# Reordering the opening transposes, filler matmuls and copies out of PSUM of an attention and feed-forward kernel

## The chip, the cores and the metric

The kernel runs on one core of one Trainium2 chip. The metric is the device time of one execution in microseconds (us). A kernel's executions are given as median and range. The profile that goes with a kernel is of one execution, and its span is about 1.8 us shorter than that execution's time, because the span begins with the first recorded instruction. All executions told of here were in the same state ("fast"); the profile gives the clock that TensorE was granted, and where it was below full speed (1.0) this is said.

In the lines of the profile PE is TensorE (matmuls), PEld its weight loads, DVE is VectorE, ACT is ScalarE, POOL is GpSimd and SP is SyncE; a `q` after an engine's name means the engine's sequencer, which issues and waits. L144 is line 144 of the kernel. PSUM is the memory that TensorE writes its results to.

## The reference

```python
def _attn_ref(x, state):                 # x (8, 8, 512, 64), state (8, 8, 32, 64)
    scores = scale * (x @ state^T);  a  = softmax(scores);   xread = a @ state
    scores2 = scale * (state @ x^T); a2 = softmax(scores2);  sread = a2 @ x
    return concat([xread, sread], axis=2)

def reference(x, state, w_in, w_out):
    y = attn.transpose(0, 2, 1, 3).reshape(8 * 544, 512)
    h = y @ w_in                         # 512 -> 2048
    g = h * sigmoid(h)
    return g @ w_out                     # 2048 -> 512
```

(Shortened to the mathematics; the maxima that the softmaxes subtract are left out.)

## The kernel before

Eight batches go through one TensorE queue. Each batch's scores need x transposed (`xT`), and the first product of the feed-forward part needs the normalised scores transposed (`aT`). For batches 0 and 1 these transposes are made by TensorE, with a copy out of PSUM behind each. For batches 2 to 7 they are made by DMA, issued from the SyncE queue. While inputs arrive, TensorE runs filler matmuls on zeros so that its clock is released (in the trace of before, at 5.63 us).

```python
def warm(n, bk, w=128):                                   # filler
    for i in range(n):
        nc.tensor.matmul(bank[bk][:, 0:w], zeros[:, 0:128], zeros[:, 0:w], ...)

def x_T(b, kt, bk):                                       # L144: x transposes on TensorE
    for c in range(4):
        nc.tensor.transpose(v[:, kt % 2, c, :], x_n[b % 2][:, kt, c, ds(2, 128)], ident[:])

def x_Te(b, kt, n, bk, eng):                              # L84 / L88: their copy
    cp(eng, xT[b % 2][:, ds(kt, n)], v[:, ds(kt % 2, n)])

def a_T(b, bks):                                          # L230: batches 0 and 1
    ...
            cp(e, aT[b % 2][:, ds(i * n, n)], v[:, ds(0, n)])

def a_Td(b):                                              # L236: batches 2 to 7
    nc.sync.dma_start_transpose(aT[b % 2]..., an[b % 2]...)

# [cut] the schedule, start of batch 0
warm(30, "o0")
# [cut]
warm(3, "w1")
x_T(0, 1, XB[1]); x_Te(0, 1, 1, XB[1], "act"); cast2(0, 3)
# [cut] loads
sc(0, 0, SB[0]);  ex(0, 0, 1, SB[0])
warm(4, "w1")
sc(0, 1, SB[1]);  ex(0, 1, 1, SB[1])
x_T(0, 2, XB[2]); x_Te(0, 2, 1, XB[2], "act")
red(0); red(1)
x_T(0, 3, XB[3]); x_Te(0, 3, 1, XB[3], "dve")
```

`sc` are scores, `ex` exponentials on ScalarE, `red` sums on VectorE of one pair of heads, and `cast2` casts one pair of heads of x as it lands.

The softmax here doesn't subtract the row's maximum and nothing guards it: scores larger than these inputs give would overflow.

Of the kernel before, what the change touches and what calls it, by code (L numbers as in the profile page):

```python
# [19 lines left out]
def kernel(  # L20
# [58 lines left out]
    def bf(name):  # L79
        return bank[name][:].bitcast(BF16)  # L80

    def cp(eng, dst, src):
        if eng == "dve":
            nc.vector.tensor_copy(dst, src)  # L84
        elif eng == "pool":
            nc.gpsimd.tensor_copy(dst, src)  # L86
        else:
            nc.scalar.activation(dst, src, func=COPY, bias=0.0)  # L88
# [43 lines left out]
    def st_f32(bk, e0, e1):  # L132
        v = bf(bk)[:, 0:128]
        for half, e in ((0, e0), (1, e1)):
            cp(
                e,
                sbd_f[ds(64 * half, 64)],
                v[ds(64 * half, 64)].rearrange("p (ns kt) -> p kt ns", kt=KT),
            )

    def x_T(b, kt, bk):
        v = bf(bk).rearrange("p (k c t) -> p k c t", k=2, c=4)
        for c in range(4):
            nc.tensor.transpose(  # L144
                v[:, kt % 2, c, :], x_n[b % 2][:, kt, c, ds(2, 128)], ident[:]
            )

    def x_Te(b, kt, n, bk, eng):
        v = bf(bk).rearrange("p (k c t) -> p k c t", k=2, c=4)
        cp(eng, xT[b % 2][:, ds(kt, n)], v[:, ds(kt % 2, n)])  # L150
# [22 lines left out]
    def sc(b, kt, bk):  # L173
        v = bank[bk][:].rearrange("p (k h c s) -> p k h c s", k=2, h=2, c=4)
        for c in range(4):
            nc.tensor.matmul(  # L176
                v[:, kt % 2, :, c, :],
                xT[b % 2][:, kt, c, :],
                sbd[:, b, kt, :, :],
                start=True,  # L180
                stop=True,
                skip_group_check=True,
            )

    def ex(b, kt, n, bk):
        v = bank[bk][:].rearrange("p (k q s) -> p k q s", k=2, q=8)
        nc.scalar.activation(  # L187
            en[b % 2][:, :, :, ds(kt, n), :].rearrange("p h c k s -> p k (h c) s"),
            v[:, ds(kt % 2, n)],
            func=EXP,  # L190
            bias=0.0,
            scale=SCALE,
        )
# [6 lines left out]
    def norm_m(b, eng, kt=0, n=4, h0=0, hn=2):  # L200
        e = nc.vector if eng == "dve" else nc.gpsimd
        e.tensor_tensor(  # L202
            an[b % 2][:, ds(h0, hn), :, ds(kt, n), :].rearrange("p h c k s -> p (h c) k s"),
            en[b % 2][:, ds(h0, hn), :, ds(kt, n), :].rearrange("p h c k s -> p (h c) k s"),
            rs[b % 2][:, ds(h0, hn), :, ds(kt, n)]
            .rearrange("p h c k -> p (h c) k")
            .unsqueeze(3)
            .to_broadcast([128, 4 * hn, n, NS]),
            op=MULT,
        )  # L210

    def norm_g(b, eng, kt, n, q0, qn):
        e = nc.vector if eng == "dve" else nc.gpsimd
        e.tensor_tensor(
            an[b % 2][:].rearrange("p h c k s -> p (h c) k s")[:, ds(q0, qn), ds(kt, n), :],
            en[b % 2][:].rearrange("p h c k s -> p (h c) k s")[:, ds(q0, qn), ds(kt, n), :],
            rs[b % 2][:]
            .rearrange("p h c k -> p (h c) k")[:, ds(q0, qn), ds(kt, n)]
            .unsqueeze(3)
            .to_broadcast([128, qn, n, NS]),  # L220
            op=MULT,
        )

    def a_T(b, bks):
        n = 2 // len(bks)
        for i, (bk, e) in enumerate(bks):
            v = bf(bk).rearrange("p (h c t) -> p h c t", h=2, c=4)
            for half in range(n):
                for c in range(4):
                    nc.tensor.transpose(  # L230
                        v[:, half, c, :], an[b % 2][:, i * n + half, c, :, :], ident[:]
                    )
            cp(e, aT[b % 2][:, ds(i * n, n)], v[:, ds(0, n)])
# [22 lines left out]
    def sread_c(b, bk, o=0, eng="act"):  # L256
        cp(eng, s_f[b % 2][:], bank[bk][:, ds(o, 2 * D + 2)])
# [21 lines left out]
    def w1_m(b, j, bks, kts=range(KT)):  # L279
        for kt in kts:  # L280
            for half in range(2):
                nc.tensor.matmul(  # L282
                    bank[bks[half]][ds(32 * kt, 32), :],
                    sbd[ds(64 * half, 64), b, kt, half, :],
                    w_in_sb[ds(64 * half, 64), kt, ds(512 * j, 512)],
                    start=True,
                    stop=True,
                    skip_group_check=True,
                    tile_position=(64 * half, 32 * kt),
                )  # L290
# [14 lines left out]
    def w1_e(b, j, bks, engs, c0=0, n=512):  # L305
        for half in range(2):
            dst = W1[b % 2][:, half, ds(512 * j + c0, n)]
            src = bank[bks[half]][:, ds(c0, n)]
            if j > 0:
                dst = dst.rearrange("p (c q) -> p c q", c=4)  # L310
                src = src.rearrange("p (q c) -> p c q", c=4)
            cp(engs[half], dst, src)
# [38 lines left out]
    def g2(b, tt, ft, bk, cols=(0, 512)):  # L351
        src = g[b % 2] if b < B else g_s
        c0, c1 = cols
        nc.tensor.matmul(  # L354
            bank[bk][:, c0:c1],
            src[:, ft, ds(128 * tt, 128)],
            w_out_sb[:, ft, c0:c1],
            start=(ft == 0),
            stop=(ft == 15),
            skip_group_check=True,  # L360
        )
# [15 lines left out]
    def warm(n, bk, w=128):  # L377
        for i in range(n):
            nc.tensor.matmul(  # L379
                bank[bk][:, 0:w], zeros[:, 0:128], zeros[:, 0:w], start=True, stop=True,  # L380
                skip_group_check=True,
            )

    with tc.manual_schedule():
# [10 lines left out]
        for i in range(2):  # L395
            nc.vector.memset(x_n[i][:, :, :, 1:131:129], 1.0)
        nc.scalar.preload_act_table(EXP)
        warm(30, "o0")

        XB = ("o0", "o1", "o0", "w1")  # L400
        SB = ("h0", "h1", "a0", "a1")
        AB = ("a0", "a1")
        HB = ("h0", "h1")
        OB = ("w0", "w1", "o0", "o1")
        DA = ("dve", "act")
        DD = ("dve", "dve")

        def G2(b, ft):
            for tt in range(4):
                g2(b, tt, ft, OB[tt])  # L410
# [23 lines left out]
        def red(kt):  # L434
            nc.vector.tensor_reduce(
                rs[0][:, :, :, ds(kt, 1)], en[0][:, :, :, ds(kt, 1), :], axis=AX, op=ADD
            )

        def rec(kt):
            v = rs[0][:, :, :, ds(kt, 2)]  # L440
            nc.vector.reciprocal(v, v)
# [6 lines left out]
        st_T(0, "w0", "dve", "dve")  # L448
        cast2(0, 2)
        st_f32("w0", "act", "dve")  # L450
        warm(3, "w1")
        x_T(0, 1, XB[1])
        x_Te(0, 1, 1, XB[1], "act")
        cast2(0, 3)
# [2 lines left out]
        load_wi(1)  # L457
        sc(0, 0, SB[0])
        ex(0, 0, 1, SB[0])
        warm(4, "w1")  # L460
        sc(0, 1, SB[1])
        ex(0, 1, 1, SB[1])
        x_T(0, 2, XB[2])
        x_Te(0, 2, 1, XB[2], "act")
        red(0)
        red(1)
        x_T(0, 3, XB[3])
        x_Te(0, 3, 1, XB[3], "dve")
        rec(0)
        norm_m(0, "pool", 0, 2)  # L470
        warm(2, "o1")
        for kt in (2, 3):
            sc(0, kt, SB[kt])
            ex(0, kt, 1, SB[kt])
# [14 lines left out]
        warm(2, "o1", 512)  # L489
        nc.scalar.preload_act_table(SILU)  # L490
        w1_e(0, 0, ("w0", "w1"), ("act", "dve"), 0, 256)
        a_T(0, (("a0", "dve"), ("a1", "act")))
        sread_c(0, "o0", 0, "dve")
        cp("act", st_nat[:, 1, :], st_f[1][:])
        load_x(1, nc.gpsimd, 2, 2)
# [53 lines left out]
        norm_s(1, 0, 2)  # L549
        norm_m(1, "pool", 0, 2)  # L550
        nc.vector.tensor_reduce(rs[1][:, :, :, 2:4], en[1][:, :, :, 2:4, :], axis=AX, op=ADD)
        nc.vector.reciprocal(rs[1][:, :, :, 2:4], rs[1][:, :, :, 2:4])
        norm_g(1, "dve", 2, 2, 0, 5)
        norm_g(1, "pool", 2, 2, 5, 3)
        G2(0, 9)
        G2(0, 10)
        w1_m(0, 3, HB)
        w1_e(0, 3, HB, ("act", "act"))
        G2(0, 11)
        sread_m(1, "a0")  # L560
        g1(0, 12)
# [164 lines left out]
```

## Time and profile before

| | before |
|---|---|
| time, median of 3 executions (range) | 215.88 us (215.65 to 216.46) |
| profiled span | 213.5 us, clock 1.0 |
| TensorE matmuls | 207.6 us busy (97%), 1666 of them |
| ScalarE, VectorE, GpSimd busy | 64%, 40%, 21% |
| DMA | 27.86 MB, mean 130 GB/s |

The prediction reads this page. The profiled execution took 215.31 us, a little less than the three in the table.

### The profile page before, as it was taken

How to read it: one execution, taken by the hardware profiler on the slowest of the kernel's cores; microseconds unless marked ns; L12 is line 12 of the kernel's file. 1: busy time of each engine (PE TensorE's matmuls, PEld its weight loads, DVE VectorE, ACT ScalarE, POOL GpSimd, SP SyncE). 2: the span in 40 equal slices, each digit the busy share in tenths (PEclk: the TensorE clock that was granted, in tenths of full speed). 3: DMA queues.
4: the chain of work that ended last, by engine and by line, in shares of the span. 5: the costliest groups of instructions: out<-in, count | busy, mean ns of one | idle time of the engine just before them, and what ended most of it. 6: DMA issues, size and time to landing. Idle time of an engine off the chain costs nothing.

```text
span 213.5 us, 4128 instructions
## 1 busy us (share of the span) xinstructions
PE 207.6 (97%) x1666; PEld 104.3 (49%) x1666; DVE 85.5 (40%) x183; ACT 135.6 (64%) x227; POOL 44.5 (21%) x86
## 2 busy tenths in 40 slices
PE   7899999999999999999999999999999999999993
PEld 7443543444454454444444545444444444566553
DVE  4883658606801664076016741382027601111110
ACT  3856686789587668883886478846885486233211
POOL 3695249003400520052005200160001000000000
PEclk9999999999999999999999999999999999999999
DMA  6999996791790197119910791165014101111112
GB/s 209 340 241 281 224 290 61 187 289 67 169 270 17 41 199 247 49 49 162 283 49 0 187 254 59 49 167 128 3 49 113 55 33 49 52 49 49 49 52 98
DMA packets 36803, 27.86 MB, mean 130 GB/s; under 512 B 22064, under 2 KB 31152, under 8 KB 36784
## 3 DMA queue, kind: packets, MB, share of 16 engines
q1 hardware_dynamic: 31872, 21.63, 35.8%
q0 software_dynamic: 4208, 5.44, 12.2%
q10 hardware_dynamic: 704, 0.52, 0.7%
q8 instruction: 13, 0.21, 0.4%
q14 instruction: 6, 0.05, 0.1%
HBM read 17.30 MB, written 8.91 MB: 123 GB/s over the span
## 4 chain that ended last, share of the span: by engine, by line
PE 93%; ACT 3%; DVE 1%; issue 1%
PE ps_o L354 28%; PE ps_w L354 26%; PE ps_h L329 26%; PE ps_h L341 3%; PE ps_o L379 2%; PE ps_a L176 1%; ACT en L187 1%; PE ps_o L282 1%; PE ps_h L282 1%; ACT W L88 1%; PE ps_o L246 1%; PE ps_a L282 1%; PE ps_a L329 1%; ACT L548 1%; PE ps_w L282 1%
## 5 line engine op out<-in xcount | busy, mean ns | idle before, releaser
L338 ACT ACTIVATE g<-ps_h 128x512 bf16<-128x512 f32 x125 | 74.1, 597 | 32.4 <-PE ps_h L329 27.9
L354 PEld LDWEIGHTS <-g 128*128 128x128 bf16 x512 | 49.0, 98 | 55.4 <-issue 2.8
L329 PE MATMUL ps_h<-aT,W 128*128 128x512 bf16 x250 | 73.5, 379 | 0.3 <-ACT W L88 0.2
L354 PE MATMUL ps_w<-w_out_sb,g 128*128 128x512 bf16 x256 | 73.0, 379 | 0.1
L354 PE MATMUL ps_o<-w_out_sb,g 128*128 128x512 bf16 x256 | 66.7, 379 | 0.1
L329 PEld LDWEIGHTS <-W 128*128 128x128 bf16 x256 | 24.3, 98 | 27.6 <-issue 1.7
L202 POOL TENSOR_TENSOR an<-en,rs 128x512 bf16<-128x512 bf16 x8 | 8.4, 1053 | 108.8 <-ACT en L187 71.3
L84 DVE COPY o_sb<-ps_w 128x512 f32<-128x512 f32 (+1 forms) x13 | 8.5, 662 | 51.5 <-PE ps_w L354 51.5
L84 DVE COPY o_sb<-ps_o 128x512 f32<-128x512 f32 x14 | 9.5, 687 | 28.6 <-PE ps_o L354 28.5
L86 POOL CAST x_u<-x_f 128x256 bf16<-128x256 f32 x44 | 17.9, 451 | 0.0
L349 ACT ACTIVATE g_s<-ps_h 128x256 bf16<-128x256 f32 x16 | 6.1, 383 | 14.0 <-PE ps_h L341 14.0
L197 DVE TENSOR_REDUCE rs<-en 128x16 f32<-128x512 bf16 x13 | 8.6, 659 | 16.0 <-ACT en L187 15.9
L341 PE MATMUL ps_h<-xsT,w_in_sb 128*128 128x256 bf16 x64 | 9.6, 273 | 0.0
L88 ACT ACTIVATE W<-ps_h 128x512 bf16<-128x512 f32 x11 | 6.5, 598 | 3.6 <-PE ps_h L282 3.6
L88 ACT ACTIVATE o_sb<-ps_o 128x512 f32<-128x512 f32 (+1 forms) x4 | 2.2, 544 | 10.3 <-PE ps_o L354 7.9
L341 PEld LDWEIGHTS <-w_in_sb 128*128 128x128 bf16 x64 | 6.9, 110 | 3.7
L187 ACT ACTIVATE en<-ps_a 128x512 bf16<-128x512 f32 (+1 forms) x16 | 8.4, 568 | 0.5 <-PE ps_a L176 0.4
L176 PEld LDWEIGHTS <-xT 128*128 128x128 bf16 x128 | 5.9, 98 | 4.6 <-ACT xT L88 1.1
L187 ACT ACT_TABLE_LOAD x6 | 7.7, 1283 | 0.1
L640 ACT ACT_TABLE_LOAD x6 | 7.7, 1283 | 0.1
L84 DVE CAST W<-ps_h 128x512 bf16<-128x512 f32 x9 | 6.2, 683 | 3.8 <-PE ps_h L282 3.8
L88 ACT ACTIVATE o_sb<-ps_w 128x512 f32<-128x512 f32 (+1 forms) x5 | 2.7, 533 | 7.8 <-issue 6.2
(90 smaller groups left out, 172.7 us busy)
## 6 DMA issues: line engine op xcount, KB each, us to landing
out_dram<-o_sb SPq DMA_DIRECT2D x32, 256.0 KB, 2.5
x_f<-in_x_dram SPq DMA_DIRECT2D x8, 512.0 KB, 4.8
x_f<-in_x_dram SPq DMA_DIRECT2D x8, 256.0 KB, 4.3
w_in_sb<-in_moe_w_in_dram POOLq DMA_DIRECT2D x3, 512.0 KB, 9.1
w_out_sb<-in_moe_w_out_dram POOLq DMA_DIRECT2D x3, 512.0 KB, 9.6
w_f<-in_moe_w_in_dram SPq DMA_DIRECT2D x2, 512.0 KB, 5.4
wo_f<-in_moe_w_out_dram SPq DMA_DIRECT2D x4, 256.0 KB, 6.3
x_f<-in_x_dram POOLq DMA_DIRECT2D x2, 512.0 KB, 7.8
```

The lines of the kernel that those rows point to most:

```text
L84: nc.vector.tensor_copy(dst, src)
L86: nc.gpsimd.tensor_copy(dst, src)
L88: nc.scalar.activation(dst, src, func=COPY, bias=0.0)
L176: nc.tensor.matmul(v[:, kt % 2, :, c, :], xT[b % 2][:, kt, c, :], sbd[:, b, kt, :, :], start=True, stop=True, skip_group_check=True,)
L187: nc.scalar.activation(en[b % 2][:, :, :, ds(kt, n), :].rearrange("p h c k s -> p k (h c) s"), v[:, ds(kt % 2, n)], func=EXP, bias=0.0, sc ...
L197: nc.vector.tensor_reduce(v, en[b % 2][:, :, :, ds(kt, n), :], axis=AX, op=ADD)
L202: e.tensor_tensor(an[b % 2][:, ds(h0, hn), :, ds(kt, n), :].rearrange("p h c k s -> p (h c) k s"), en[b % 2][:, ds(h0, hn), :, ds(kt, n), ...
L282: nc.tensor.matmul(bank[bks[half]][ds(32 * kt, 32), :], sbd[ds(64 * half, 64), b, kt, half, :], w_in_sb[ds(64 * half, 64), kt, ds(512 * j, ...
L329: nc.tensor.matmul(bks[i][:], W1[b % 2][:, half, ds(128 * (f0 + i), 128)], aT[b % 2][:, half, :, :], start=(half == 0), stop=(half == 1), ...
L338: nc.scalar.activation(g[b % 2][:, f0 + i, :], bks[i][:], func=SILU, bias=0.0)
L341: nc.tensor.matmul(bk[:, 0:256], wi_cols(kt, ft), xsT[:, kt, :, :, :], start=(kt == 0), stop=(kt == KT - 1), skip_group_check=True,)
L354: nc.tensor.matmul(bank[bk][:, c0:c1], src[:, ft, ds(128 * tt, 128)], w_out_sb[:, ft, c0:c1], start=(ft == 0), stop=(ft == 15), skip_group ...
```

## The change

Its intent is to shorten the relay between the engines at the start (5.8 to 9.1 us) by letting transposes run earlier and keeping a copy from standing behind a sum, and to remove a wait near 31 us. The fillers are changed along with it.

```diff
-        warm(30, "o0")
+        warm(8, "o0", 512)
 # [cut]
-        warm(3, "w1")
+        warm(1, "w1", 256)
 # [cut]
-        warm(4, "w1")
+        x_T(0, 2, XB[2])
+        x_Te(0, 2, 1, XB[2], "act")
         sc(0, 1, SB[1])
         ex(0, 1, 1, SB[1])
-        x_T(0, 2, XB[2])
-        x_Te(0, 2, 1, XB[2], "act")
         red(0)
-        red(1)
         x_T(0, 3, XB[3])
         x_Te(0, 3, 1, XB[3], "dve")
+        red(1)
+        warm(1, "o1", 256)
         rec(0)
         norm_m(0, "pool", 0, 2)
-        warm(2, "o1")
+        warm(1, "o1", 256)
 # [cut]
-        a_T(0, (("a0", "dve"), ("a1", "act")))
+        a_T(0, (("a0", "act"), ("a1", "dve")))
 # [cut] batch 1, about 30 us in ("part 2" of the prediction)
+        G2(0, 9)
+        G2(0, 10)
+        w1_m(0, 3, HB)
+        w1_e(0, 3, HB, DA)
         nc.vector.reciprocal(rs[1][:, :, :, 2:4], rs[1][:, :, :, 2:4])
         norm_g(1, "dve", 2, 2, 0, 5)
         norm_g(1, "pool", 2, 2, 5, 3)
-        G2(0, 9)
-        G2(0, 10)
-        w1_m(0, 3, HB)
-        w1_e(0, 3, HB, ("act", "act"))
```

Of small fillers there were 30 + 3 + 4 + 2 = 39; there are 8 + 1 + 1 + 1 = 11. That is 28 fewer, or 56 instructions of TensorE.

## The prediction

> **What bounds the kernel now.** I read the page's totals and its chain of waits first, then the chain in order of time from 0 to 60 us, then the timeline of each engine from 0 to 16 and from 26 to 42 us, and last each transfer's time to landing. The page says that TensorE has work for 97% of the span, and the chain says the same:
>
> ```profile
> PE 93%; ACT 3%; DVE 1%; issue 1%
> ```
>
> So nothing outside TensorE's queue is worth much, and the change must be read where that chain leaves TensorE. It does so in few places. Two of them are touched by the diff, and these are the pieces of the chain there (start us, length us, engine, what it writes, line):
>
> ```profile
> 1.19 3.38 PE ps_o L379 x30
> 4.57 0.43 PE ps_o L144 x4
> ...
> 5.83 0.27 ACT sbd_f L88
> 6.10 0.49 ACT xT L88
> 6.59 0.05 issue
> 6.63 0.30 PE ps_h L176 x4
> 6.94 0.02 issue
> 6.96 0.39 ACT en L187
> 7.36 0.02 issue
> 7.38 0.42 DVE rs L435
> 7.80 0.03 issue
> 7.83 0.44 DVE xT L84
> 8.27 0.05 issue
> 8.31 0.30 PE ps_a L176 x4
> 8.62 0.02 issue
> 8.64 0.39 ACT en L187
> 9.04 0.04 issue
> 9.08 0.42 PE ps_o L246 x28
> ...
> 30.14 1.09 ACT W L88 x2
> 31.24 0.04 issue
> 31.28 0.59 PE ps_h L329 x2
> ```
>
> L379 are filler matmuls on zeros, L144 the x transposes, L176 scores, L187 exponentials, L435 sums of a pair of heads, L84 and L88 copies on VectorE and ScalarE, L246 the state read, L329 the first product of the feed-forward part. What to see: from 5.8 to 9.08 us TensorE waits for a relay in which the copy of the fourth x transposes (7.83) stands behind the second sum (7.38), which itself had to wait for the second exponential (6.96). The copy needs neither; it stands there only because VectorE runs in order. From 9.08 to 25.8 us the chain is TensorE alone, so what comes earlier at 9.08 comes earlier later, unless something new gets in between. At 30.14 two copies of weights run one after the other on ScalarE, because its table load ends only at 30.13, and TensorE waits 0.22 us for the second (its timeline: idle 0.22 before 31.28).
>
> **What the Trainium skill says.** Three places bear on it. "TensorE: Matmul & The Clock Gate", Part 1: a cold array issues a matmul every N / 1.2 GHz (106.7 ns for 128 columns, 426.7 ns for 512), a warm one at twice the rate, and the window that releases it is about 3.4 us of activity, free-running. The trace agrees on spacing: 30 fillers of 128 columns start at 1.19 us and the next transpose at 4.36, 105.7 ns each. Single matmuls of 128 columns last 314 ns until about 5.8 us and 219 ns after, so the release came 4.6 us after the first filler. "PSUM — Partial Sum Buffer", PSUM bank collisions raise a hardware error: two engines must not touch one bank at the same time, reads against reads included. The schedule obeys that: ScalarE's `sbd_f` copy at 5.83 waits for VectorE's two `sbd` copies from the same bank, which end at 5.73. "ScalarE: Activation LUTs", What ACT_TABLE_LOAD costs: back-to-back ACTIVATEs overlap by about 93 ns. Here two exponentials take 0.87 us where one takes 0.38 and there is a wait between; of the second copy of `xT`, 6.00 to 6.58, the last 0.10 lies beside the next exponential at 6.48. I use 0.1.
>
> **Part 1, the start.** The opening filler goes from 30 x 105.7 = 3.17 us to 8 x 426.7 = 3.41 us. The inputs of the first transposes are cast by 4.04 (GpSimd's 3.52 + 0.52), so they waited for the filler already, and now wait 0.24 us more: 4.60 instead of 4.36. The second filler shrinks from 3 x 0.107 = 0.32 to 0.21 us, but the relay behind the state's transpose (sbd copies, sbd_f, second xT copy) carries the whole 0.24: sbd_f 6.07 to 6.34, second `xT` copy 6.24 to 6.82 instead of 6.00 to 6.58.
>
> From there the new order. ScalarE: first exponential 6.72 to 7.10, third `xT` copy (0.58) 7.00 to 7.58, second exponential 7.48 to 7.86. VectorE: first sum 7.12 to 7.54, at once the fourth `xT` copy (0.42) to 7.92. TensorE: third scores from 7.63, fourth from 7.97 (they started 7.89 and 8.31). Exponentials three and four: 7.97 to 8.35 and 8.30 to 8.68, against 9.03 before. Net of the 0.24 lost, 0.35 us earlier; without the longer filler it would be about 0.6.
>
> Not all of it arrives. After the state read TensorE has 0.59 (first half of L295) and two 512-column fillers, 0.43, then the transposes of the normalised scores (L230). So TensorE could be there at 8.72 + 0.42 + 0.59 + 0.43 = 10.16 instead of 10.51. Their inputs: the second sum is now behind the fourth copy, 7.89 to 8.31, then reciprocal 8.27 to 8.51, and GpSimd's product of 1.05 us starts 0.17 later, at 8.68 (before: 8.58), ends 9.73, and its small product of 0.71 ends at about 10.47 (before 10.62, when it waited for the second reciprocal). VectorE's sums, reciprocal and product end at about 10.15 (before 10.36). First four transposes at 10.20, last four at 10.50; the second half of L295 starts at about 10.75 against 11.04. **About 0.29 us** stays. The swap of the two copies out of L230 (the first to ScalarE, 0.60, the second to VectorE, 0.43) ends both at about 11.4; before, ScalarE ended the second at 11.75. But TensorE reached the matmul that needs the second half at 12.07, 0.3 us later, so the swap in itself is worth zero now; it removes a wait that would come up if the rest were faster by more than 0.3.
>
> **Part 2, around 30 us.** One of the two weight copies moves from ScalarE to VectorE, in front of a reciprocal. VectorE's sum ends at 29.90 and its source (L282, ended about 29.73) is there: 29.87 to 30.56. ScalarE's remaining copy: 30.14 to 30.73. TensorE ends the state read of batch 1 at 31.05 and no longer waits: 0.22 gained. The price: reciprocal 30.53 to 30.78, VectorE's product (0.68) to 31.50 instead of 30.89, GpSimd's (0.75) 30.84 to 31.59 instead of 31.27. The transposes that read them can be reached at 31.06 + 0.43 = 31.49, so they wait some 0.05. **About 0.2 us** stays.
>
> Sum: 0.29 + 0.20 = 0.49, about 0.5 us of 215.88: 215.4.
>
> **The rivals.** (a) A transfer hides the gain of the start. The first half of `w_f`, issued at 3.60, lands 5.0 us later; the second, issued at 4.20, 5.8 us later, at 10.0, wanted at 10.75. The weights used at 16.12, 21.17 and 29.32 land at 15.5, 20.6 and 28.5 (issue plus time to landing). Least slack about 0.6, so a shift of 0.3 fits; if the landings slip, it is 215.7. (b) GpSimd takes the place of the wait removed: its product starts later although everything else starts earlier. By the times above the transposes wait for it from about 10.42 to 10.50, counted already; were its product slower by 0.2, the front would give 0.1 and the total 0.3: 215.6. (c) The clock is released later. The relay now has fewer fillers, and the release came at 5.8, with TensorE busy throughout; my times keep it busy until about 5.8 too. If the release slips past the small matmuls, each of some 40 of 64 and 128 columns up to 9 us costs 25 to 50 ns more, half of them on the relay: 0.5 to 1 us lost, 215.9 to 216.4. If on the contrary the longer fillers release it sooner, the relay gains some 0.2: 215.2. (d) Nothing arrives because later waits are fixed in time. The chain from 31.28 on is TensorE with waits that start from TensorE (52.30, 53.44), so I hold this unlikely; 215.9.
>
> **Range and chances.** I take 215.4. The kernel before scattered from 215.65 to 216.46 in three runs, more than the effect. (a), (b) and half of (c) together make 215.6 to 216.1; both parts in full with an earlier clock make 214.9. Hence 214.8 to 216.1 for 8 in 10. Two per cent is 4.3 us, more than the whole relay from 5.8 to 9.08; only an unknown fault could reach it in either direction: 0.01 each.
>
> **What would show it right or wrong.** In the changed kernel's trace the first x transposes should start at about 4.6; the fourth exponential should end at about 8.7; the transposes of the normalised scores should start near 10.2 with a short wait for GpSimd in their middle; the first L329 matmul near 11.35 (before 11.64); the L329 matmul after the second state read should have no idle time before it, and start some 0.5 earlier than 31.28. From there every piece should be shifted by the same 0.5. It is wrong if 314 ns matmuls go on past 6.5 us (rival c), if L295 waits for a transfer (a), if the transposes wait over 0.2 us for GpSimd (b, or the price of part 2 at 31.5), or if the shift at 31 us is gone by 60.

## More of the kernel before

One `warm(1, ...)` is two instructions of TensorE: a weight load and a matmul.

One part of the page was not read before the prediction, the table of DMA queues (queue and kind, then packets, MB, and share of the 16 engines' time):

```profile
q1 hardware_dynamic: 31872, 21.63, 35.8%
...
q8 instruction: 13, 0.21, 0.4%
```

The second line is instructions, fetched by DMA while the program runs: 13 packets, which the trace lists at 16,384 bytes each.

## The result, and the profile after

| | before | after |
|---|---|---|
| time, median (range), 4 executions each | 215.76 us (215.65 to 216.46) | 217.31 us (216.77 to 217.39) |
| profiled span | 213.5 us | 215.6 us, clock 0.992 |
| TensorE busy, matmuls | 207.6 us, 1666 | 208.3 us, 1638 |

The changed kernel took 1.0060 times as long, with a 95% interval of 1.0032 to 1.0087. A ratio is always the mean time of one kernel's fast runs over that of the other's from the same rounds, so it isn't quite the ratio of the medians. The predicted gain of 0.5 us had become a loss of about 1.3 us, outside the range. The executions at clock 1.0 and 0.998 took 217.28 and 216.77 us, so the clock isn't the main reason. The two profiled executions lie further apart than the kernels do, 215.31 us before and 217.39 after, so part of what their traces differ in is chance.

The summary of the chain of waits, after, now has waits for DMA in it (before, the prediction's first line has none):

```profile
PE 89%; DMA 5%; SPq 1%; issue 1%; DVE 1%; ACT 1%; POOL 0%; POOLq 0%; ACTq 0%
```

I divided the span by two landmarks that both kernels have: the SyncE queue issues the DMA transpose `aT<-an` for batch 2 and, later, for batch 3. The first is issued at 53.20 us before and at 54.28 after, the second at 73.78 and 75.89. From the second to a store near the end (at 163.51 and 165.63 us) both kernels take 89.7 us. So of 2.1 us, **1.08 lie before the first issue and 1.03 between the two; nothing lies after**.

**The front.** The chain after, in order of time (start, length, what):

```profile
3.57 7.05 DMA w_f<-in_moe_w_in_dram
10.62 0.04 issue
10.66 0.83 PE ps_w L295 x16
```

The timeline of TensorE after (start, length, engine, line, operation; in brackets the idle time before, and what ended it):

```profile
6.96 0.40 PE L144 MATMUL ps_o<-ident,x_n 128*128 128x128 bf16 x4 [1.13 <-POOL x_n L86]
7.19 0.28 PE L176 MATMUL ps_h<-sbd,xT 128*128 128x64 bf16 x4
7.61 0.59 PE L144 MATMUL ps_w<-ident,x_n 128*128 128x128 bf16 x4
...
10.66 0.83 PE L295 MATMUL ps_w<-w_f,sbd_f 64*32 64x256 f32 x16 [0.46 <-DMA w_f<-in_moe_w_in_dram]
```

The third x transposes, which now stand ahead of the second scores, wait 1.13 us for the cast of the third piece of x, which landed later than in the trace of before. Then L295 waits 0.46 us more for the weights. The first product (L329) starts at 13.00 us instead of 11.64, 1.36 later; the piece near 31 us takes 0.28 of that back, which leaves 1.08.

**The middle.** TensorE near 57 us, first before, then after:

```profile
56.73 0.59 PE L329 MATMUL ps_h<-aT,W 128*128 128x512 bf16 x2
```

```profile
57.38 0.59 PE L354 MATMUL ps_w<-w_out_sb,g 128*128 128x512 bf16 x2
58.70 0.61 PE L329 MATMUL ps_h<-aT,W 128*128 128x512 bf16 x2 [0.73 <-DMA aT<-an]
```

Nothing near 57 us was changed, and yet there is a new wait of 0.73 us for the DMA transpose issued at 54.28. The transfers from 52 to 59 us, in 40 slices of 0.175 us (tenths of the engines' busy time, then the rate), show why. Before:

```profile
DMA  0040000000000199999999996000599999999999
GB/s 0 0 94 0 0 0 0 0 0 0 0 0 0 34 209 221 211 217 196 209 284 386 386 410 234 0 0 0 127 227 221 214 203 214 208 214 222 221 227 217
...
q8 instruction: 1, 0.02, 1.2%
```

After:

```profile
DMA  8000000000000000000099999998000000999999
GB/s 340 24 0 0 0 0 0 0 0 0 0 0 0 0 0 0 0 0 0 15 186 221 214 205 297 200 99 3 0 6 7 10 9 15 375 433 410 386 163 193
...
q8 instruction: 1, 0.02, 0.9%
```

Before, the third slice holds 94 GB/s for 0.175 us, 16.4 KB: that is the instruction packet, at 52.35 us, while nothing else moves. The transpose runs from slice 14 on and lands 3.1 us after its issue. After, the packet starts at 56.22 us (the 25th slice), in the middle of the transpose. Then nearly everything stops for seven slices, 1.2 us, in which the rate is 0 to 15 GB/s, and the transpose lands 4.4 us after its issue. That is what TensorE waits for.

### The profile page after: what moved, and what is told of

Same layout as the page of the kernel before. It is cut to its first block, busy times and chain, and to the rows that moved or that the text cites. A ratio compares the mean times of both kernels' runs of the same rounds, so it can differ in the third digit from the quotient of the medians.

```text
span 215.6 us, 4083 instructions
## 1 busy us (share of the span) xinstructions
PE 208.3 (97%) x1638; PEld 102.0 (47%) x1638; DVE 85.4 (40%) x184; ACT 135.1 (63%) x226; POOL 44.8 (21%) x86
## 4 chain that ended last, share of the span: by engine, by line
PE 89%; DMA 5%; SPq 1%; issue 1%; DVE 1%; ACT 1%; POOL 0%; POOLq 0%; ACTq 0%
PE ps_o L354 27%; PE ps_h L329 25%; PE ps_w L354 25%; DMA w_f<-in_moe_w_in_dram 3%; PE ps_h L341 3%; DMA aT<-an 2%; PE ps_a L176 2%; PE ps_h L282 1%; SPq L96 1%; PE ps_o L282 1%; PE ps_a L282 1%; PE ps_w L295 1%; PE ps_a L329 1%; PE ps_o L246 1%; ACT L187 1%
## 5 line engine op out<-in xcount | busy, mean ns | idle before, releaser
L329 PE MATMUL ps_h<-aT,W 128*128 128x512 bf16 x250 | 73.5, 379 | 0.8 <-DMA aT<-an 0.7
L329 PEld LDWEIGHTS <-W 128*128 128x128 bf16 x256 | 24.1, 98 | 28.6 <-issue 2.0
L84 DVE CAST W<-ps_h 128x512 bf16<-128x512 f32 x10 | 6.8, 683 | 4.0 <-PE ps_h L282 4.0
L88 ACT ACTIVATE W<-ps_h 128x512 bf16<-128x512 f32 x10 | 6.0, 597 | 3.6 <-PE ps_h L282 3.6
```

The lines of the kernel that those rows point to most:

```text
L84: nc.vector.tensor_copy(dst, src)
L88: nc.scalar.activation(dst, src, func=COPY, bias=0.0)
L329: nc.tensor.matmul(bks[i][:], W1[b % 2][:, half, ds(128 * (f0 + i), 128)], aT[b % 2][:, half, :, :], start=(half == 0), stop=(half == 1), ...
```

## The experiments

The theories have the letters of the expectations. The first call tested three. **O:** the new order, the swap or part 2 brings the loss, for instance by making TensorE wait for pieces of x. **F:** the opening filler is to blame. **M:** it is scatter, slow transfers in some executions of any kernel. For the second call the traces of the first split F in two. **N:** having fewer TensorE instructions moves an instruction fetch into the DMA transpose of `aT`, which then stalls. **D:** the opening filler's duration or width does harm by itself, through the clock or the front. The calls went to three different chips (one for e1, one for e2, one for e3), each with runs of the kernel before beside it.

### First call: copies, and the opening filler exchanged

Unchanged copies of both kernels (no edit):

> The kernel before, unchanged, once more, so that its trace comes from the same chip and hour as the other three. Theory O (the new order of the x transposes makes TensorE wait for pieces of x) and theory F (the longer opening filler is to blame): 215.7, ratio 1.000, first half of w_f landing about 5 us after its issue. Theory M (input transfers are slow in some executions, whatever the kernel, and the change only met such a one): its trace shows w_f landing 6.5 us or more after issue, and its time is 216.5 or more.

> The changed kernel, unchanged, once more. O and F: again 217.0 to 217.4, ratio 1.006, and again TensorE idle about 1 us before the third x transposes and half-rate matmuls (over 0.3 us for 128 columns) between 7.5 and 11 us. M: the time falls back to between 215.3 and 215.8 if this execution's transfers are as fast as those of the kernel before.

The copy of before took 215.35 us (215.30 to 217.66), ratio 0.9999 [0.9956, 1.0043]. The copy of after took 217.05 us (216.03 to 217.84), ratio 1.0049 [1.0013, 1.0085]. The loss is there in another call, so M does not explain it. In the new trace of after the first product starts at 11.89 us, not 13.00, and the half-rate matmuls that O and F expected are not there (clock 1.0): the front had been mostly bad luck of landing times. But a later load of weights cost it 0.8 us, and the pause and the 0.7 us wait for `aT` were there again.

The changed kernel with the old opening:

```diff
-        warm(8, "o0", 512)
+        warm(30, "o0")
```

> The changed kernel with only the opening filler as it was: 30 matmuls of 128 columns instead of 8 of 512. F: the loss is gone, 215.3 to 215.6. O: still 216.8 to 217.4, since the order is still the new one. M: follows the transfers alone.

It took 215.82 us (215.24 to 217.98), ratio 1.0006 [0.9963, 1.0048]. `aT` lands 3.0 us after issue, and TensorE doesn't wait for it. The loss is gone, with all the rest of the change still in; the median is 0.2 us above the range that F gave. O, which expected 216.8 or more, falls as the main cause.

The kernel before with the new opening:

```diff
-        warm(30, "o0")
+        warm(8, "o0", 512)
```

> The kernel before with only the opening filler as in the change: 8 matmuls of 512 columns. F: 216.8 to 217.4. O: 215.6 to 216.0, the 0.24 us by which the filler is longer at most. M: follows the transfers alone.

It took 216.13 us (216.01 to 216.82), ratio 1.0016 [0.9986, 1.0046]. The ratio is not clear of 1, but the trace has the pause; `aT` lands 3.9 us after issue, and TensorE waits at the same line:

```profile
57.35 0.60 PE L329 MATMUL ps_h<-aT,W 128*128 128x512 bf16 x2 [0.27 <-DMA aT<-an]
```

So the opening filler alone brings the pause, here a milder one: the median missed the 216.8 or more that F expected, and the segment between the two `aT` issues takes 21.02 us against 20.57 before and 21.61 after. Whether the filler does it by its duration or by its number of instructions is the next question.

### Second call: duration against number, and the parts alone

Changed kernel; as long as 8 x 512 columns, but with 22 matmuls more:

```diff
-        warm(8, "o0", 512)
+        warm(30, "o0", 136)
```

> The changed kernel with an opening filler of 30 matmuls of 136 columns: as long as the change's 8 of 512 (30 x 113 = 8 x 427 = 3.4 us), but as many instructions as before. Theory N (the number of TensorE instructions shifts the 16 KB instruction fetches into the DMA transposes at about 55 to 58 us): the fetch lies before the transposes' data moves (at 52.5 to 53.8 us), TensorE waits less than 0.2 us for aT there, and the time is 215.6 to 216.2, at most 0.25 above the 30 x 128 variant's 215.82. Theory D (the duration of the filler, or the clock's release, is what costs): 216.8 to 217.4, and a wait for aT of about 0.7 us.

It took 215.91 us (215.35 to 216.65), ratio 0.9993 [0.9956, 1.0029]. `aT` lands 3.2 us after issue and TensorE does not wait for it, although in this trace the clock was released only at 10.59 us. The line of TensorE, with no idle time before it, and the transfers from 52 to 59.5 us:

```profile
57.31 0.59 PE L329 MATMUL ps_h<-aT,W 128*128 128x512 bf16 x2
GB/s 0 0 0 0 0 0 0 0 0 0 87 0 0 0 0 14 187 225 205 72 22 168 292 213 0 0 273 404 350 229 152 193 235 212 202 203 228 217 212 214
```

The packet (87) comes 0.1 us after the issue, and the data start only later; they have a short dip (72, 22) and no pause. D falls: the duration is the same and the loss is gone.

Kernel before; as long as 30 x 128 columns, but with 22 matmuls fewer:

```diff
-        warm(30, "o0")
+        warm(8, "o0", 480)
```

> The kernel before with an opening filler of 8 matmuls of 480 columns: as long as its own 30 of 128 (3.2 us), with 44 instructions fewer. N: the fetch moves to about 54.5 us, TensorE waits 0.2 to 0.8 us for aT at 57 us, 215.9 to 216.3. D: 215.4 to 215.7, no wait for aT.

It took 216.98 us (216.54 to 217.20), ratio 1.0039 [1.0008, 1.0071]. With nothing changed but the number and width of filler matmuls, `aT` lands 4.7 us after issue, and TensorE waits 1.0 us, more than N expected (215.9 to 216.3, 0.2 to 0.8 us):

```profile
58.31 0.61 PE L329 MATMUL ps_h<-aT,W 128*128 128x512 bf16 x2 [1.04 <-DMA aT<-an]
```

The transfers of this run from 52 to 59 us:

```profile
GB/s 0 0 0 0 0 0 0 0 0 0 0 0 0 0 0 18 281 203 203 118 10 0 0 0 0 3 9 9 10 10 237 293 364 398 410 269 265 202 215 214
```

The packet starts at 54.87 us, and after 118 come ten slices of 10 GB/s or less. The pair of these two kernels is the test that decides between N and D.

Kernel before with part 2 alone (the last two hunks of the diff):

> The kernel before with only the second part of the change (one weight copy to VectorE in front of a reciprocal at 30 us). Its own step of the prediction: the 0.22 us of idle time before the product at 31.3 us is gone, 0.2 us faster than before in the same rounds (about 215.2 at the fast end). If the later reciprocal holds up the transposes of batch 1, or another wait absorbs it, 0.0.

It took 216.08 us (215.08 to 216.46), ratio 0.9994 [0.9959, 1.0028]. Part 2 does no harm, and its gain is hidden in the scatter.

Kernel before with part 2 and only the fourth x transposes and their copy moved in front of the second sum:

```diff
         red(0)
-        red(1)
         x_T(0, 3, XB[3])
         x_Te(0, 3, 1, XB[3], "dve")
+        red(1)
```

> The kernel before with the second part and only the fourth x transposes of the first part (in front of the second sum), third ones left behind the second scores, fillers and instruction count as before. If the wait for the third piece of x is what eats the gain of the new order (theory O, second form): fourth exponential ends 0.2 to 0.4 us earlier than in the kernel before, no wait over 0.3 us for a piece of x, 214.9 to 215.3 at the fast end. If the relay is bound by the fourth piece of x as well: no better than part 2 alone.

It took 215.60 us (215.28 to 217.51), ratio 0.9997 [0.9956, 1.0039]. The state read at 8.79 us is no earlier than in before (8.75): in this trace the transposes waited 0.26 us for the cast of the fourth piece of x. My expectation of the front was missed.

### Third call: openings in between, order and swap

Changed kernel with two openings of the same total width, between 8 and 30 in number:

```diff
-        warm(8, "o0", 512)
+        warm(16, "o0", 256)
```

> The changed kernel with an opening filler of 16 matmuls of 256 columns: the change's duration (16 x 213 = 3.4 us), 8 filler matmuls more than the change, 14 fewer than the 30 x 136 variant. Theory N (instruction fetch inside the DMA transposes): from the 8-matmul kernel (fetch 1.8 to 1.9 us after the issue of aT) to the 30-matmul one (0.1 us after) each matmul moves the fetch by about 0.08 us, so here it begins about 1.2 us after the issue, when transpose data is moving: TensorE waits 0.3 to 1.0 us for aT, 216.4 to 217.2. Rival (the filler's width or anything of the start matters): a time between, about 216.3, with no wait for aT.

```diff
-        warm(8, "o0", 512)
+        warm(24, "o0", 171)
```

> The changed kernel with an opening filler of 24 matmuls of 171 columns: same duration again. N: the fetch begins about 0.6 us after the issue of aT, before its data starts to move (about 1.1 us after the issue): no wait for aT above 0.2 us, 215.6 to 216.2. If already a fetch that overlaps the first of that data stops it, 216.3 or more, and the border lies nearer to the 30-matmul variant.

With 16 fillers: 216.74 us (216.17 to 217.66), ratio 1.0030 [0.9985, 1.0076]; the pause is there, `aT` lands 4.3 us after issue, and TensorE waits 0.7 us, as N expected. With 24: 215.70 us (215.17 to 216.55), ratio 0.9981 [0.9941, 1.0020]; 3.4 us and no wait, again as expected. The transfers of 52 to 59 us with 24 fillers:

```profile
GB/s 0 0 0 0 0 0 0 0 0 0 0 0 94 0 0 98 211 206 190 47 16 10 168 293 256 3 0 222 445 374 246 211 98 228 219 212 206 217 218 221
```

The packet (94) comes just before the transpose's data (98 and on), and only a short dip follows, 47, 16 and 10.

Kernel before with the swapped copies alone:

```diff
-        a_T(0, (("a0", "dve"), ("a1", "act")))
+        a_T(0, (("a0", "act"), ("a1", "dve")))
```

> The kernel before with only the two copies of the transposed scores on swapped engines. By the prediction's step this is worth zero: the copy that ends last ends about 0.2 to 0.3 us earlier, and no idle time of TensorE goes away. 215.4 to 216.0, ratio 0.998 to 1.002.

It took 216.63 us (215.31 to 217.54), ratio 1.0018 [0.9974, 1.0061], above the expected 215.4 to 216.0, but a scatter of this size says nothing on so small an effect. The trace does. TensorE in this run:

```profile
10.16 0.67 PE L295 MATMUL ps_w<-w_f,sbd_f 64*32 64x256 f32 x16 [0.66 <-DMA w_f<-in_moe_w_in_dram]
...
11.20 0.61 PE L230 MATMUL ps_a<-ident,an 128*128 128x128 bf16 x8
...
12.34 1.04 PE L329 MATMUL ps_h<-aT,W 128*128 128x512 bf16 x4
```

Weights came late here, before the swapped copies have a part. From the transposes to the product it is 12.34 - 11.20 = 1.14 us; before, 11.64 - 10.51 = 1.13. The swap is worth zero.

Kernel before with the new order and the new small fillers, but the opening of 30 x 128, no swap, and no part 2:

> The kernel before with only the new order of the third and fourth x transposes and the small fillers that go with it (opening 30 x 128 as before, 12 instructions fewer, no swap, no second part). By the prediction's step: first product of the feed-forward part 0.4 to 0.5 us earlier than before (0.29 plus what the longer filler costs). If TensorE waits for the third piece of x in front of the second scores, as the traces so far have it: 0.1 to 0.2 us later than in the copy of before (11.66), ratio 1.000 to 1.002; no wait for aT above 0.2 us.

It took 216.05 us (215.08 to 217.13), ratio 0.9993 [0.9950, 1.0037]. The state read starts at 8.47 us, 0.28 earlier than in before. The product starts at 11.98 and not earlier, because L295 waited 0.51 us for weights.

### What the runs say together

Start of the fetch and landing of `aT` are counted from the issue of the first `aT` transpose; the segment is from that issue to the next `aT` issue.

| kernel | small fillers fewer | fetch start | `aT` landing | segment |
|---|---|---|---|---|
| before, its copy, swap only | 0 | -0.85 to -1.02 | 3.1 | 20.57 to 20.58 |
| order only | 6 | +0.17 | 3.0 | 20.58 |
| part 2 only, fourth and part 2 | 0 | -0.97, -0.98 | 3.0, 3.1 | 20.69, 20.70 |
| after with 30 x 128, 30 x 136 | 6 | +0.11, +0.09 | 3.0, 3.2 | 20.70, 20.71 |
| after with 24 x 171 | 12 | +0.71 | 3.4 | 20.71 |
| after with 16 x 256 | 20 | +1.26 | 4.3 | 21.57 |
| before with 8 x 512, 8 x 480 | 22 | +1.19, +1.29 | 3.9, 4.7 | 21.02, 21.79 |
| after, its copy | 28 | +1.94, +1.76 | 4.4, 4.3 | 21.61, 21.56 |

The first column is worked out from the programs, the others from one trace of each kernel. Two things follow. The fewer instructions there are ahead of it, the later the fetch comes relative to the program, though not in even steps: the first 6 move it by about 1.1 us, the next 22 by about 1.7. (Number and width change together in most openings, but 30 x 136 leaves the fetch where 30 x 128 has it, and order only moves it with the opening untouched.) And the full pause is in all five traces in which the fetch came 1.19 to 1.94 us after the issue, when the transpose's data are moving, and in none of the other nine.

The same traces hold five more `aT` transposes each, for later batches, 84 in all. Whenever a fetch started 1.19 to 2.35 us after an issue, nine times, the transpose landed 3.9 to 4.7 us after it. Four of these nine are the second transpose (about 74 us) in the kernels with 6 or 12 fillers fewer, which have no pause at the first: after with 30 x 128 has a fetch 2.02 us after that issue and the landing at 4.43. With no fetch near (43 times) they landed after 3.0 to 3.1 us. With a fetch 2.4 to 3.2 us after the issue they landed after 3.0 to 3.1 as well, 22 times of 23 (8 x 480 has the exception, 4.75). So the pause goes with where the fetch falls, and not with the kernel's opening as such. At those four TensorE did not wait.

The number of instructions can be seen in the trace as well. Busy times from the start to the first `aT` issue of before and then of after (stretch, its length, then PE, PEld, DVE, ACT and POOL with numbers of instructions, the clock, the DMA's share, GB/s):

```profile
0.00:53.20 53.20, 50.74 (x486) 25.90 (x486) 31.37 (x73) 37.88 (x64) 23.89 (x42) 1.00 0.88 220
```

```profile
0.00:54.28 54.28, 51.11 (x458) 23.79 (x458) 31.20 (x74) 37.40 (x63) 24.14 (x42) 0.97 0.88 215
```

TensorE reaches the same point of the program after 486 matmuls in before and after 458, 28 fewer, in after. In the 14 traces the fetch starts when TensorE has started 454 to 481 weight loads. Counted from the `aT` issue, it starts 16 to 32 loads ahead with no filler fewer, 1 behind with 6 fewer and 9 behind with 28 fewer. So the fetch keeps its place in the count of instructions roughly, while the transpose keeps its place in the work: that is why the two slide past each other. By what rule a fetch is started is not shown; the count isn't exact (481 with 6 fewer, 467 with 28).

The times agree with the traces. The kernels with the pause have 28 executions, mean 216.83 us, of which none is below 216.0. The changed kernel with 24 or 30 fillers has 18, mean 215.93, of which 10 are below 216.0; the kernel before has 43, mean 216.02, of which 28 are.

No version here beats the kernel before beyond the scatter. The changed kernel with 24 x 171 fillers is the best candidate, but its interval includes 1.

## Why the prediction was wrong, point by point

**The failing step** is "From there every piece should be shifted by the same 0.5", together with the dismissal of rival (d) because the waits after 31.28 us "start from TensorE". The wait at 57 us is for a DMA transpose, whose duration depends on when instructions are fetched, and that depends on the number of instructions ahead. I worked out the fillers' durations and not their number. Measured in its place: `aT` lands up to 1.6 us later (4.7 against 3.1), and the segment takes 21.56 and 21.61 us instead of the 20.70 that the same code takes without the pause, about 0.9 us lost. Without the pause the changed code's mean, 215.93 us, lies in the predicted range, but the gain of 0.5 isn't there either (216.02 before); the points below say where it went.

The Trainium skill, "Runtime: NRT & Kernel Launch", Instruction fetch mechanics, states that the instruction memory is refilled in blocks of 16 KiB, 256 instructions, by a DMA queue that the engine's sequencer drives itself, and that the cost of a block is mostly hidden. I had not looked it up. The traces agree on the block: 13 packets of 16,384 bytes, and before's 1666 matmuls with as many weight loads are 3,332 instructions, by an estimate from that page's figure 13.0 blocks. That this queue serves TensorE is inferred from this and from the fetch's shift; the trace doesn't name its engine. On the cost no run here decides for TensorE's own issue: no wait of TensorE is put down to instructions, but the profile has no such label. The cost of 0.9 us comes through another transfer.

**The front, "about 0.29 us stays".** The mechanism was right and its size was in part a matter of luck. With x landing early, as with 24 x 171, the state read starts at 8.50 us against 8.75, and the product at 11.53 against 11.64, so 0.11 of the predicted 0.29 arrived. The fourth exponential ended as predicted (8.78 against 8.7), but VectorE's product behind it took 0.70 us where before's took 0.56, and ended at 10.25 instead of 10.15 (before 10.36). It decides: in 13 of 14 traces TensorE's wait for the operands of L230 ends 0.03 to 0.04 us after that product. Why it took longer is open. Besides, I took the landing times of one trace as fixed. Over 14 traces of both kernels and their variants the first half of `w_f` landed 4.8 to 7.1 us after its issue, and TensorE waited for one of the halves in six (0.3 to 1.0 us). The cast of the third piece of x started at 5.33 us in before's trace but at 6.1 to 6.4 in nine others, and the transposes that now stand ahead of the scores waited for it, up to 1.13 us. So rival (a) did come true, by the trace's luck and in both kernels; weights for later products were late in some traces as well, by up to 1.3 us (swap only). This may be what makes up the scatter of executions, which one trace of each kernel can't show.

**The longer filler, 0.24 us.** The 3.41 us behind it is an estimate from the figure of the page that the prediction cites. Confirmed as 0.22 where the clock was cold throughout: the first x transposes start at 4.58 us in the copy of after and in before with 8 x 512, against 4.36 in before. By itself it did no harm (30 x 136).

**Rival (c), the clock.** In 12 of the 14 traces the clock was released at 3.9 to 6.7 us, without a pattern by kernel (before's at 5.63, which the prediction read as 5.8 from the matmuls); swap only has no record of it, and in 30 x 136 it is 10.59. In the profiled run of after it was throttled again from 7.67 to 11.08 us, following the 1.13 us wait; transposes at 7.61 took 0.59 us instead of 0.40. That span is 3.41 us, the window that the prediction cites from "TensorE: Matmul & The Clock Gate", Part 1. It may have added to the front of that execution, but isn't the loss: runs at full clock have it too.

**The swap, "worth zero now".** Confirmed: 1.14 against 1.13 us.

**Rival (b).** The transposes of the scores didn't come to wait for GpSimd by 0.2 us in the profiled run of after; weights held the chain there. Where they didn't (24 x 171), the transposes waited for VectorE's product, as said under the front (the profile names GpSimd's, which had ended at 9.84).

**Part 2, "about 0.2 us stays".** TensorE after with the opening of 30 x 128:

```profile
30.79 0.43 PE L246 MATMUL ps_a<-x_n,en 128*32 128x65 bf16 x32
31.15 0.60 PE L329 MATMUL ps_h<-aT,W 128*128 128x512 bf16 x2
```

From the state read to the product it takes 0.36 us here with no idle time; before, 30.62 to 31.28 is 0.66. That is 0.30, a little more than predicted. But every kernel with part 2 takes 20.69 to 20.71 us in the later segment where those without take 20.57 to 20.58, in the absence of the pause: 0.12 is given back between 59 and 74 us, in three steps of some 0.04 us that I did not trace further. The net of 0.16 to 0.18 is too small for these runs to confirm as a time.

**What stays open.** Why a fetch stalls a DMA transpose in flight is not shown, only when it does. Why no time is lost at the second transpose, which lands as late in five traces, was not traced either (8 x 480 loses some 0.2 us there). Whether the longer opening makes weights land later on average can't be told from these few traces.

## What to carry to other kernels

Filler instructions and any others ahead of a critical transfer have two sizes, their duration and their number: when you change filler, keep the number and change the width, or look at where the instruction fetches fall among DMA transposes, before and after. Take landing times from several traces, not one, before counting on a slack of half a microsecond; moving work forward in an in-order queue makes everything behind it wait for its input on the unlucky executions (1.13 us in the run after). When a change at the start ends in a loss, divide the span at landmarks that both kernels have, and see in which stretch the time goes before explaining any of it.

## What the Trainium skill lacked or had wrong

- "Runtime: NRT & Kernel Launch", Instruction fetch mechanics, calls the cost of a block "mostly hidden". It lacks that a fetch can stall a DMA transpose: transfers nearly stop for about 1 us (0 to 15 GB/s in the run after), the transpose lands 3.9 to 4.7 us after issue instead of 3.0 to 3.4, and the kernel loses about 0.9 us. It also lacks the consequence that removing 22 filler matmuls shifts such a fetch by some 2 us (-0.85 to +1.19) against the work.
- "DMA: Bandwidth & Descriptors", Rules for kernel authors, says of correctness that a DMA transpose next to ordinary DMAs needs nothing; all outputs here were correct. Neither there nor in its section DMA Transpose (X-bar) is there a word on what an instruction fetch does to a transpose's time, in the numbers above.
- No page that I looked up gives the scatter of a load's landing between executions: the same half of `w_f` landed 4.8 to 7.1 us after its issue.
